# Norm's last step and the split of the score maxima on VectorE, earlier row loads and other turn slots in a four-layer FNet and sliding-window attention kernel

## Chip, cores and metric

One core of a Trainium2 chip. The metric is the device time of one execution in microseconds (us). The kernel before takes 2400.96 us, the median of 3 runs (2399.59 to 2403.11).

## What is computed

Four layers on x of 2048 rows by 640 columns, in fp32: FNet mixing, attention, FNet mixing, attention, each behind a layer norm and with a residual.

```python
def _A_ref(x, dft_seq_re, dft_seq_im, dft_hid_re, dft_hid_im):
    a = jnp.einsum("bsd,ed->bse", x, dft_hid_re)
    b = jnp.einsum("bsd,ed->bse", x, dft_hid_im)
    return jnp.einsum("ts,bse->bte", dft_seq_re, a) - jnp.einsum("ts,bse->bte", dft_seq_im, b)

def _B_ref(x, wqkv, wo):                      # H = 32 heads of 20, window W = 256
    ...
    scores = jnp.einsum("bhqd,bhkd->bhqk", q, k) * (Dh ** -0.5)
    mask = (idx[:, None] - idx[None, :] >= 0) & (idx[:, None] - idx[None, :] < W)
    p = _softmax(jnp.where(mask[None, None], scores, -1e9), axis=-1)
    o = jnp.einsum("bhqk,bhkd->bhqd", p, v)
    return (lambda x, *d: x.transpose(*d))(o, 0, 2, 1, 3).reshape(B, S, D) @ wo

x = x + _A_ref(_layernorm(x), ...)
x = x + _B_ref(_layernorm(x), B_wqkv, B_wo)
x = x + _A_ref(_layernorm(x), ...)
x = x + _B_ref(_layernorm(x), B_wqkv, B_wo)
```

## The kernel before

Products are made in fp16 on TensorE (PE), each fp32 operand split into a high and a low part, with three products for one. The FNet layers (`spectral`) take 0 to 605 us and 1290 to 1788 us. The change lies in the attention layers (`attention`), whose slots take 605 to 1232 us and 1788 to 2375 us.

**Slots.** An attention layer runs 256 slots g: 8 blocks of 256 rows (b), 32 slots r each; a slot is one tile of 128 query rows for one pair of heads. In slot g

- `scores(g)` (L1026) writes the scores of the slot to the bank `sp` (one buffer); VectorE (DVE) masks them (L1043) and takes the largest of each query into `m` (L1047).
- `by_key(g - 7)` (L1071) makes the scores of an earlier slot again, keys on the partitions, in the bank `tp` (one buffer); the largest scores come in as two more rows of the stack `qs`. ScalarE (ACT) takes the exponential into `ptq` (L1092); GpSimd (POOL) cuts the window's edges out (L1097, L1099).
- Every fourth slot: `values` multiplies by v, `back` (L1129) transposes and divides (L1140 to L1144).

**Maxima.** Of four slots 4n to 4n+3 one `m` holds the maxima. `part_tops(n)`, in slot 4n+4, splits them on GpSimd into a high and a low part in `tops` (L1053 to L1055). `hand_on(n)`, at the end of that slot, transposes `tops` on TensorE into the bank `pt`, and `copy_tops` has ScalarE copy that into rows of `qs` (L1069).

**Fill.** Between these stand the products of the projections and of the output (`proj_qk`, `proj_v`, `out_tile`, bank `pf`), cut to single matmuls. `run_fill(ns)` issues so many ns of them in a slot, by a rate that spreads the rest over the layer. A `turn` (`turned`, L936) is five transposes of a 128x640 tile into the bank `pt`, which has one buffer and is shared with `hand_on`, and a copy out of it by ScalarE (L947) or VectorE (L945). `turn_unit` issues at most one in a slot. `flush(kind)` issues all that is left of a kind at a deadline, and first ends the unit under way.

**Norms.** A norm (`norm_steps`, L118) is cut to steps of a few VectorE instructions; `slow_step` issues one in a slot, behind that slot's reduction (`tc.issue_after(topped[0])`). Its last step writes `lny` (L147); then `split` casts it on ScalarE (`xs`, L159) and takes the low part on GpSimd (L160). `rows_norm(b + 2)` makes so the rows that the projections of a later block read (two tiles, both layers, blocks 2 to 7); its rows are loaded from `x2_d` on SP's queue, in slot r = 13 (`VALUE_LAG`), just ahead of the first step. `next_norm` (first attention layer only) does the same for a finished output tile. Loads, and the stores of `qkd` with the loads of `qs` and `ks` behind them, share SP's queue, in order.

The order of each engine's instructions comes from the tile framework, from the order and the constraints of the code.

Of the kernel before, what the change touches and what calls it, by code (L numbers as in the profile page):

```python
# [42 lines left out]
HAND_LAG = 4  # L43
# [3 lines left out]
M_UP = 2.0 ** 15  # L47
SHIFT = -20.0
TURN_STEPS = 8
X_UP = 2.0 ** 10  # L50
C_UP = 2.0 ** 8
W_UP = 2.0 ** 13
# [6 lines left out]
def body(ctx: ExitStack, tc: tile.TileContext, x_in, cmat, whid, wqkv, wo, out):  # L59
# [55 lines left out]

    matmul, transpose = partial(tensor, "matmul"), partial(tensor, "transpose")

    def norm_steps(xs, ys, eng=nc.vector):  # L118

        n = len(xs)  # L120
        mv = keep.tile([P, n, 2], F32, tag=f"lnmv{n}", name="lnmv", bufs=2)
        for k, x in enumerate(xs):
            st = keep.tile([P, 2, 6], F32, tag="lnst", name="lnst", bufs=2)
            for h in range(2):
                nc.vector.bn_stats(st[:, h], x[:, h * 320:(h + 1) * 320])
                if h == 0:
                    yield
            nc.vector.bn_aggr(mv[:, k], st.rearrange("p a b -> p (a b)"))
            yield
        t = keep.tile([P, 3, n], F32, tag=f"lnt{n}", name="lnt", bufs=2)  # L130
        v, g, u = t[:, 0], t[:, 1], t[:, 2]
        nc.vector.tensor_scalar(v, mv[:, :, 1], 1e-5, X_UP ** -2, op0=OP.add, op1=OP.mult)
        nc.vector.tensor_scalar(g.bitcast(I32), v.bitcast(I32), 1, None, op0=OP.logical_shift_right)
        nc.vector.tensor_scalar(v, v, -0.5, None, op0=OP.mult)
        nc.vector.tensor_scalar(g.bitcast(I32), g.bitcast(I32), -1, 0x5F3759DF, op0=OP.mult, op1=OP.add)
        yield
        for k in range(3):
            if n == 1:
                nc.vector.scalar_tensor_tensor(u, g, v, g, op0=OP.mult, op1=OP.mult)
            else:  # L140
                nc.vector.tensor_tensor(u, g, g, op=OP.mult)
                nc.vector.tensor_tensor(u, u, v, op=OP.mult)
            nc.vector.scalar_tensor_tensor(g, u, 1.5, g, op0=OP.add, op1=OP.mult)
            yield
        for k, x in enumerate(xs):
            y = keep.tile([P, D], F32, tag="lny", name="lny", bufs=2)
            normed[0] = eng.tensor_scalar(y, x, mv[:, k, 0:1], g[:, k:k + 1],  # L147
                                                op0=OP.subtract, op1=OP.mult).ins
            ys.append(y)
            yield  # L150
# [608 lines left out]
    def attention(layer, proj, dst, final):  # L759
        with ExitStack() as st:  # L760
# [135 lines left out]

            def next_norm(i, x3):
                ys = []
                yield from norm_steps([x3], ys, nc.gpsimd)
                xs = new_xs()  # L900
                split(xs[:, 0], xs[:, 1], ys[0], nc.gpsimd)
                xt = keep.tile([P, 2, ND, P], F16, tag="xto", name="xto", bufs=2)
# [19 lines left out]
            def rows_norm(b, x2s):  # L922

                ys = []
                yield from norm_steps(x2s, ys, nc.gpsimd)
                for t, y in enumerate(ys):
                    xs = new_xs()
                    split(xs[:, 0], xs[:, 1], y, nc.gpsimd)
                    live[-1].extend(rows_turn(b, xs, t, k) for k in range(2))
                    fill.extend(Unit(now[0] + TURN_STEPS // 2, g, ("rows", b), now[0], [], True) for g in live[-1])  # L930
                    yield

            def rows_turn(b, xs, t, k):
# [75 lines left out]
                return sum(max(u.ns, 0) for u in fill + [unit[0]] if u is not None and u.kind in kinds) - credit[0]  # L1009

            def flush(kind):
                while any(u.kind == kind for u in fill) or (unit[0] and unit[0].kind == kind):
                    if unit[0] is None:
                        unit[0] = min((u for u in fill if u.kind == kind), key=lambda u: u.due)
# [34 lines left out]
            def part_tops(n):  # L1049

                m, hl = TOP.pop(n), tops[n % 2]
                u = sb.tile([P, 4, 2], F32, tag="u", name="u", bufs=2)
                nc.gpsimd.tensor_scalar(u, m, -1.0 / M_UP, None, op0=OP.mult)  # L1053
                nc.gpsimd.tensor_copy(hl[:, :, 0:66:64], u)
                nc.gpsimd.tensor_tensor(hl[:, :, 1:66:64], u, hl[:, :, 0:66:64], op=OP.subtract)  # L1055

            def hand_on(n):

# [135 lines left out]
            for g in range(NS):  # L1194
                now[0] = g
                b, r = divmod(g, 2 * NP)
                if g < NG:
                    if r == 0:
                        flush(("qk", b))
                        flush(("rows", b + 1))  # L1200
                        if b < NBQ - 1:
                            queue_qk(b + 1)
                            queue_v(b + 1)
                    scores(g)
                if 0 <= g - KEY_LAG < NG:
                    by_key(g - KEY_LAG)
                if g < NG and r == VALUE_LAG:
                    flush(("v", b))
                    if b < NBQ - 2:
                        proj.new_rows(b + 2)  # L1210
                        x2s = [keep.tile([P, D], F32, tag="res", name="x2", bufs=4) for t in range(2)]
                        for t in range(2):
                            load(x2s[t], x2_d[2 * (b + 2) + t])
                        slow.append(rows_norm(b + 2, x2s))
                    if b == NBQ - 1 and not final:
                        hidden = Hidden(xu_d)
                        hidden.load()
# [3 lines left out]
                for pi in range(2):  # L1221
                    n, m = divmod(g - HAND_LAG - 1 - pi, 4)
                    if m == 0 and 0 <= n < NG // 4:
                        copy_tops(n, pi)
                n, m = divmod(g - HAND_LAG, 4)
                if m == 0 and 0 <= n < NG // 4:
                    part_tops(n)
                slow_step()
                n, m = divmod(g - VALUE_LAG, 4)
                if m == 0 and 0 <= n < NG // 4:  # L1230
# [7 lines left out]
                    rate = max(rate, left(("v", b)) / (VALUE_LAG - r))  # L1238
                if g < NG and r < QK_SLOT:
                    rate = max(rate, left(("v", b), ("qk", b + 1)) / (QK_SLOT - r))  # L1240
                if (g - HAND_LAG) % 4 in (0, 3) or g >= NG + HAND_LAG:
                    turn_unit()
                run_fill(max(rate, 400) * FILL[(g - VALUE_LAG + 2) % 4])
                n, m = divmod(g - HAND_LAG, 4)
                if m == 0 and 0 <= n < NG // 4:
                    hand_on(n)
# [41 lines left out]
```

## Time and profile before

| | |
|---|---|
| runs, median of 3 | 2400.96 us |
| profiled execution, time | 2404.99 us |
| profiled execution, span of the core | 2403.3 us |
| mean granted TensorE clock over the span | 0.97 |
| GpSimd norm steps (L147) | 40, 102.3 us |
| GpSimd split of the maxima (L1053 to L1055) | 3 x 128, 31.0 + 27.1 + 28.6 us |
| ScalarE exponential (L1092) | 512, 486.2 us |

A profile line of a wait reads: who waited, for whom, us in total, how often, the longest. A line of the timeline reads: start, duration, engine, line, operation, tile written and tiles read, shapes, and in brackets how long the engine had been idle and what ended that. "PEld" is TensorE's weight load, "PEclk" the granted clock as a share of full speed. The lines of kernel.py that a profile names are those of the kernel before.

### The profile page before, as it was taken

The page shows a single profiled execution, that of the slowest core. Times are in us where ns is not written, and L with a number is a line of the kernel's source. Part 1 is how long each engine was busy: PE and PEld are TensorE (multiplying, and loading weights), DVE is VectorE, ACT ScalarE, POOL GpSimd, SP SyncE. Part 2 cuts the span into 40 slices and gives each one's busy share as a digit, 9 for nine tenths or more (in the row PEclk, how much of TensorE's full clock was granted, in tenths as well). Part 3 has the DMA queues.
Part 4 walks back from the last instruction along what each step waited for, and adds up shares of the span by engine and source line. Part 5 has one row for each costly group of instructions (what it writes and reads, how often), then busy time and mean ns, then how long its engine had stood idle before and what let it go on. Part 6 is the DMA issues. An engine that isn't in the chain of part 4 may idle for free.

```text
span 2403.3 us, 55464 instructions
## 1 busy us (share of the span) xinstructions
PE 2169.1 (90%) x21985; PEld 1515.7 (63%) x21985; DVE 1621.3 (67%) x3305; ACT 1267.7 (53%) x2120; POOL 1539.1 (64%) x2197
## 2 busy tenths in 40 slices
PE   7999899989898888889888999999987899889997
PEld 5667566667565566566556777777665566666664
DVE  7887979676666666666656758585766565656564
ACT  5334443432576666666654433434325666666775
POOL 5666758565557676666556858585746655665554
PEclk9999999999999999999898999999999999999999
DMA  5854556275330332133314545464542321232130
GB/s 179 287 203 157 200 176 204 90 255 140 95 86 31 83 96 63 49 91 85 128 57 141 192 136 192 136 202 169 197 109 68 85 56 56 70 85 62 53 90 23
DMA packets 187609, 292.98 MB, mean 122 GB/s; under 512 B 13908, under 2 KB 120660, under 8 KB 178004
## 3 DMA queue, kind: packets, MB, share of 16 engines
q1 hardware_dynamic: 157108, 223.55, 31.0%
q10 hardware_dynamic: 30240, 65.88, 7.4%
q8 instruction: 172, 2.82, 0.5%
q14 instruction: 89, 0.73, 0.1%
HBM read 202.51 MB, written 86.87 MB: 120 GB/s over the span
## 4 chain that ended last, share of the span: by engine, by line
PE 58%; DVE 17%; POOL 9%; DMA 7%; issue 5%; ACT 3%; SPq 0%; DVEq 0%; ACTq 0%; POOLq 0%
PE pf L112 23%; PE y L112 8%; PE pv L112 6%; PE z L112 6%; PE x L112 6%; DVE cc L482 5%; PE sp L112 4%; POOL lny L147 3%; DVE m L1047 2%; PE tp L112 2%; PE pt L112 2%; DVE sp L1043 2%; ACT ptq L1092 2%; DMA x<-x2d 1%; DVE res L505 1%
## 5 line engine op out<-in xcount | busy, mean ns | idle before, releaser
L112 PEld LDWEIGHTS <-cc 128*128 128x128 f16 x5376 | 528.0, 99 | 243.4 <-issue 38.8
L1092 ACT ACTIVATE ptq<-tp,shift,alpha 128x768 f32<-128x768 f32 (+2 forms) x512 | 486.2, 950 | 212.5 <-PE tp L112 199.5
L112 PEld LDWEIGHTS <-big 128*128 128x128 f16 x4320 | 413.2, 99 | 144.5 <-issue 31.1
L1043 DVE COPY_PREDICATED sp<-mask,sp 128x256 f32<-128x256 int32 x448 | 191.4, 427 | 292.4 <-PE sp L112 277.9
L1047 DVE TENSOR_REDUCE m<-sp 128x2 f32<-128x512 f32 (+1 forms) x512 | 344.8, 673 | 25.6 <-POOL os L1143 0.5
L1097 POOL TENSOR_SCALAR_AFFINE_SELECT ptq<-ptq 128x512 f32<-128x512 f32 x224 | 142.8, 637 | 284.3 <-ACT ptq L1092 274.3
L112 PE MATMUL pf<-early,big 128*128 128x256 f16 x2400 | 312.2, 277 | 1.1 <-ACT qf L328 1.1
L479 ACT ACTIVATE cc<-cs 128x512 f16<-128x512 f32 x256 | 152.3, 623 | 254.6 <-POOL cs L472 103.5
L112 PE MATMUL y<-zc,cc 128*128 128x320 f16 x1728 | 265.3, 301 | 13.7 <-DVE pf L505 13.7
L112 PE MATMUL pf<-big 128*128 128x320 f16 x1680 | 243.4, 303 | 12.2 <-DVE early L250 5.4
L482 DVE SCALAR_TENSOR_TENSOR cc<-cs,cc 128x512 f16<-128x512 f32 x256 | 232.3, 923 | 4.9 <-ACT cc L479 4.9
L482 DVE SCALAR_TENSOR_TENSOR cc<-cq,cc 128x512 f16<-128x512 f32 x192 | 201.2, 1049 | 0.0
L112 PE MATMUL pv<-ptq,v 128*32 128x128 f32 (+1 forms) x3840 | 191.2, 340 | 0.0
L112 PE MATMUL z<-zc,cc 128*128 128x320 f16 x1152 | 180.5, 302 | 8.4 <-DVE res L505 8.4
L112 PE MATMUL tp<-qs,ks 62*128 62x128 f16 x2688 | 153.9, 221 | 33.9 <-ACT ptq L1092 32.8
L1099 POOL TENSOR_SCALAR_AFFINE_SELECT ptq<-ptq 128x512 f32<-128x512 f32 x256 | 164.7, 643 | 29.1 <-ACT ptq L1092 28.3
L112 PE MATMUL x<-zc,cc 128*128 128x320 f16 x1152 | 182.7, 303 | 0.0
L112 PE MATMUL sp<-ks,qs 62*128 62x256 f16 (+1 forms) x1792 | 155.2, 252 | 29.3 <-DVE m L1047 28.1
L112 PEld LDWEIGHTS <-ks 62*128 62x128 f16 x3008 | 119.0, 96 | 82.4 <-issue 51.2
L112 PE MATMUL pf<-big,early 128*128 128x320 f16 x960 | 160.1, 308 | 3.7 <-DVE x L872 3.7
L1069 ACT ACTIVATE qs<-pt 2x512 f16<-2x512 f16 x224 | 131.4, 586 | 54.1 <-PE pt L112 50.4
L112 PEld LDWEIGHTS pv<-ptq,v 128*32 128x32 f32 x3840 | 110.4, 113 | 59.9 <-issue 8.2
(146 smaller groups left out, 3654.7 us busy)
## 6 DMA issues: line engine op xcount, KB each, us to landing
cq<-in_cmat_dram SPq DMA_DIRECT2D x64, 1024.0 KB
accd<-res ACTq DMA_DIRECT2D x96, 320.0 KB
res<-accd SPq DMA_DIRECT2D x96, 320.0 KB
x<-x2d SPq DMA_DIRECT2D x64, 320.0 KB
qkd<-early SPq DMA_DIRECT2D x160, 128.0 KB
ks<-qkd SPq DMA_DIRECT2D x108, 160.0 KB
qs<-qkd SPq DMA_DIRECT2D x84, 160.0 KB
x2d<-res ACTq DMA_DIRECT2D x32, 320.0 KB
```

What stands on the lines that cost most here:

```text
L112: i = getattr(nc.tensor, what)(*args, **kw)
L147: normed[0] = eng.tensor_scalar(y, x, mv[:, k, 0:1], g[:, k:k + 1], op0=OP.subtract, op1=OP.mult).ins
L479: nc.scalar.activation(cc[m][:, 0], f, AF.Copy, scale=C_UP)
L482: nc.vector.scalar_tensor_tensor(cc[m][:, 1], f, C_UP, cc[m][:, 0], op0=OP.mult, op1=OP.subtract)
L505: marks["dve"] = nc.vector.scalar_tensor_tensor(o, z, Y_DOWN, f, op0=OP.mult, op1=OP.add).ins
L1043: nc.vector.copy_predicated(sp[:, :, 2 * P:3 * P], mask[:, None, :].to_broadcast([P, 2, P]), far)
L1047: topped[0] = nc.vector.tensor_reduce(TOP[g // 4][:, g % 4], sp[:, :, c0:3 * P], axis=AX.X, op=OP.max).ins
L1069: nc.scalar.activation(o, handed[n][rs].rearrange("r (i p) t -> r i p t", i=2), AF.Copy)
L1092: nc.scalar.activation(q[:, h:h + 2, a0 + first:a0 + 3], tp[:, :, first * P:3 * P].rearrange("p a (b c) -> p a b c", c=P), AF.Sigmoid, bia ...
L1097: nc.gpsimd.affine_select(out=q[:, :, a0], in_=q[:, :, a0], pattern=[[0, 4], [-1, P]], base=0, channel_multiplier=1, compare_op=OP.is_gt, ...
L1099: ins = nc.gpsimd.affine_select(out=q[:, :, a0 + 2], in_=q[:, :, a0 + 2], pattern=[[0, 4], [1, P]], base=0, channel_multiplier=-1, compare ...
```

## The change

It has four parts.

- The last step of a norm (`lny`) is always VectorE's; in the attention layers it was GpSimd's.
- The maxima are split by two VectorE instructions, straight from `m`, in slot 4n+3 behind its reduction, where three GpSimd instructions did it in slot 4n+4. The steps of the norms wait for the second of them, too.
- The rows for `rows_norm` are loaded in slot r = 4 and not 13, and the norm starts in slot r = 9 and not 13. Their turns may come three and not four slots behind the norm.
- A turn is issued in slots 4n+3, and in slots 4n (in which `hand_on` follows) only if over 1000 ns of products come behind it; before in both. `flush` issues turns of the kind first, and does not end the unit under way for them.

```diff
+TURN_ROOM = 1000
+NORM_STEPS = (4, 9)
+ROW_STEPS = 3
...
-    def norm_steps(xs, ys, eng=nc.vector):
+    def norm_steps(xs, ys):
...
-            normed[0] = eng.tensor_scalar(y, x, mv[:, k, 0:1], g[:, k:k + 1],
+            normed[0] = nc.vector.tensor_scalar(y, x, mv[:, k, 0:1], g[:, k:k + 1],
                                                 op0=OP.subtract, op1=OP.mult).ins
...
-                yield from norm_steps([x3], ys, nc.gpsimd)
+                yield from norm_steps([x3], ys)
...
-                yield from norm_steps(x2s, ys, nc.gpsimd)
+                yield from norm_steps(x2s, ys)
...
-                    fill.extend(Unit(now[0] + TURN_STEPS // 2, g, ("rows", b), now[0], [], True) for g in live[-1])
+                    fill.extend(Unit(now[0] + ROW_STEPS, g, ("rows", b), now[0], [], True) for g in live[-1])
...
             def flush(kind):
+                for u in sorted((u for u in fill if u.kind == kind and u.turn), key=lambda u: u.due):
+                    fill.remove(u)
+                    while step(u):
+                        pass
                 while any(u.kind == kind for u in fill) or (unit[0] and unit[0].kind == kind):
...
                 m, hl = TOP.pop(n), tops[n % 2]
-                u = sb.tile([P, 4, 2], F32, tag="u", name="u", bufs=2)
-                nc.gpsimd.tensor_scalar(u, m, -1.0 / M_UP, None, op0=OP.mult)
-                nc.gpsimd.tensor_copy(hl[:, :, 0:66:64], u)
-                nc.gpsimd.tensor_tensor(hl[:, :, 1:66:64], u, hl[:, :, 0:66:64], op=OP.subtract)
+                hi = hl[:, :, 0:66:64]
+                nc.vector.tensor_scalar(hi, m, -1.0 / M_UP, None, op0=OP.mult)
+                topped[0] = nc.vector.scalar_tensor_tensor(hl[:, :, 1:66:64], m, -1.0 / M_UP, hi, op0=OP.mult, op1=OP.subtract).ins
...
                     scores(g)
+                    if g % 4 == 3:
+                        part_tops(g // 4)
                 if 0 <= g - KEY_LAG < NG:
                     by_key(g - KEY_LAG)
+                if g < NG and b < NBQ - 2:
+                    if r == NORM_STEPS[0]:
+                        x2s = [keep.tile([P, D], F32, tag="res", name="x2", bufs=4) for t in range(2)]
+                        for t in range(2):
+                            load(x2s[t], x2_d[2 * (b + 2) + t])
+                    if r == NORM_STEPS[1]:
+                        slow.append(rows_norm(b + 2, x2s))
                 if g < NG and r == VALUE_LAG:
                     flush(("v", b))
                     if b < NBQ - 2:
                         proj.new_rows(b + 2)
-                        x2s = [keep.tile([P, D], F32, tag="res", name="x2", bufs=4) for t in range(2)]
-                        for t in range(2):
-                            load(x2s[t], x2_d[2 * (b + 2) + t])
-                        slow.append(rows_norm(b + 2, x2s))
...
-                n, m = divmod(g - HAND_LAG, 4)
-                if m == 0 and 0 <= n < NG // 4:
-                    part_tops(n)
                 slow_step()
...
-                if (g - HAND_LAG) % 4 in (0, 3) or g >= NG + HAND_LAG:
+                ns = max(rate, 400) * FILL[(g - VALUE_LAG + 2) % 4]
+                m = (g - HAND_LAG) % 4
+                if m == 3 or m == 0 and credit[0] + ns > TURN_ROOM or g >= NG + HAND_LAG:
                     turn_unit()
-                run_fill(max(rate, 400) * FILL[(g - VALUE_LAG + 2) % 4])
+                run_fill(ns)
```

Three places of the program show how instructions move. The line numbers of the change's rows are its own.

**The norm of two tiles of rows, block 3 of the second attention layer.** GpSimd before (`x_27226` and `x_27227` are the rows, `qf` a projection's result):

```order
L329 CAST early<-qf 128x256
L147 TENSOR_SCALAR lny<-x_27226,lnmv,lnt 128x640
L330 TENSOR_TENSOR early<-qf,early 128x256
L147 TENSOR_SCALAR lny<-x_27227,lnmv,lnt 128x640
L160 TENSOR_TENSOR xs<-lny,xs 128x640 x2
L1097 AFFINE_SELECT ptq<-ptq 128x4x128
```

VectorE in the change, in the same block (`x_26713` and `x_26714` are the same rows):

```order
L150 TENSOR_SCALAR lny<-x_26713,lnmv,lnt 128x640
L1050 COPY_PREDICATED sp<-mask,sp 128x2x128
L1054 TENSOR_REDUCE m<-sp 128x2
L150 TENSOR_SCALAR lny<-x_26714,lnmv,lnt 128x640
L1050 COPY_PREDICATED sp<-mask,sp 128x2x128
L1054 TENSOR_REDUCE m<-sp 128x2
L1146 RECIPROCAL r<-pv 128x8
L1060 TENSOR_SCALAR tops_77<-m 128x4x2
L948 COPY ot<-pt 128x640
L1061 SCALAR_TENSOR_TENSOR tops_77<-m,tops_77 128x4x2
L1147 TENSOR_TENSOR o<-pv,r 128x160
```

The two steps `lny` leave GpSimd's queue and stand in VectorE's, one behind the reduction of a slot each, in two slots that follow each other. The last rows are a slot 4n+3, in which the two instructions on `tops` stand between the reduction and the next slot's masking copy, with those of `back` and a turn's copy among them.

**SP's queue around the load of rows, second attention layer.** Before (`x_27226`, `x_27227` are rows for a norm, `x_27321` a residual of an output tile, `qkd_1` the stores of k):

```order
L168 DMA qs<-qkd_0_153 20x16x256 x6
L168 DMA qkd_1_156<-early 128x2x256 x2
L168 DMA x_27226<-x2d_89 128x640
L168 DMA x_27227<-x2d_90 128x640
L168 DMA qkd_1_156<-early 128x2x256
L168 DMA x_27321<-x2d_83 128x640
```

In the change (`x_26713` and `x_26714` are those rows, `x_26676` and `x_27147` residuals):

```order
L171 DMA qs<-qkd_0_153 20x16x256 x6
L171 DMA x_26676<-x2d_82 128x640
L171 DMA x_26713<-x2d_89 128x640
L171 DMA x_26714<-x2d_90 128x640
L171 DMA qkd_1_156<-early 128x2x256 x3
L171 DMA x_27147<-x2d_83 128x640
```

The load of the rows stood behind the second store of k of its block, and now stands ahead of the first.

**TensorE in the first slot of block 4, second attention layer.** Before (`os` is a tile that is turned, `tops_78` the split maxima):

```order
L112 MATMUL pt<-idh,os 128x128
L112 LDWEIGHTS os
L112 MATMUL pt<-idh,os 128x128
L112 LDWEIGHTS tops_78
L112 MATMUL pt<-idh,tops_78 66x128
```

In the change (`early` are rows, `pf` the bank of a projection):

```order
L115 MATMUL pf<-big,early 128x320
L115 LDWEIGHTS early
L115 MATMUL pf<-big,early 128x320
L115 LDWEIGHTS tops_78
L115 MATMUL pt<-idh,tops_78 66x128
```

In before a turn stood directly ahead of the transposes of `tops`, and no product in that slot; in the change no turn stands in it and six products come ahead of them.

## Prediction

> **What bounds the kernel now.** I read the page first, for who is busy, and then the busy times by stretch, cut at the two attention layers (605 to 1232 us and 1788 to 2375 us) and the FNet layer between them.
>
> ```profile
> PE 2169.1 (90%) x21985; PEld 1515.7 (63%) x21985; DVE 1621.3 (67%) x3305; ACT 1267.7 (53%) x2120; POOL 1539.1 (64%) x2197
> ```
> ```profile
> core 0: us, PE busy (x) PEld busy (x) DVE busy (x) ACT busy (x) POOL busy (x), PEclk, DMA share, GB/s
> 605.00:1232.00 627.00, 546.84 (x7002) 373.89 (x7002) 408.89 (x1010) 412.90 (x622) 406.29 (x776) 0.96 0.28 78
> ...
> 1290.00:1788.00 498.00, 487.25 (x3615) 352.47 (x3614) 347.79 (x543) 187.27 (x377) 346.19 (x291) 1.00 0.51 170
> 1788.00:2375.00 587.00, 523.69 (x6761) 358.17 (x6760) 362.11 (x802) 387.16 (x578) 349.30 (x743) 0.96 0.25 66
> ```
>
> The FNet layer leaves TensorE (PE) idle for 498.0 - 487.3 = 11 us, at full clock. The attention layers leave it idle for 80 and 63 us, and there the granted clock is 0.96. The change touches the attention layers alone (the one shared function, `norm_steps`, is called elsewhere with VectorE already), so what it can gain lies in those 143 us and in the missing 0.04 of the clock. Next are TensorE's waits, first of 605 to 1232 us, then of 1788 to 2375 us (us in total, times, longest):
>
> ```profile
> PE sp L112 <- DVE m L1047: 17.7, 21, 2.3
> PE tp L112 <- ACT ptq L1092: 16.8, 16, 3.5
> PE pt L112 <- POOL tops L1055: 9.6, 9, 2.0
> PE pt L112 <- ACT xto L947: 7.3, 5, 3.4
> PE pt L112 <- DVE ot L945: 6.3, 5, 1.7
> PE pt L112 <- ACT xs L159: 5.7, 1, 5.7
> PE pt L112 <- ACT early L947: 4.1, 6, 1.1
> PE pt L112 <- ACT ot L947: 3.9, 5, 1.6
> ```
> ```profile
> PE sp L112 <- DVE m L1047: 21.0, 29, 2.2
> PE tp L112 <- ACT ptq L1092: 20.5, 10, 4.4
> PE pt L112 <- DVE ot L945: 5.4, 5, 1.1
> PE pt L112 <- POOL tops L1055: 5.4, 4, 4.3
> PE pt L112 <- DVE early L945: 2.8, 7, 0.6
> ```
>
> No single wait rules. There are four families: the bank `tp` that ScalarE (ACT) empties late, the bank `sp` that VectorE (DVE) empties late, the maxima that GpSimd (POOL) splits late, and the bank `pt` that holds a finished turn. To see why ScalarE is late I followed one of the longest, in the timeline of the second attention layer (TensorE, ScalarE, GpSimd):
>
> ```profile
> 2062.92 0.34 PE L112 MATMUL sp<-ks,qs 62*128 62x128 f16 x4
> 2066.94 0.50 PE L112 MATMUL tp<-qs,ks 62*128 62x128 f16 x6 [3.68 <-ACT ptq L1092]
> ```
> ```profile
> 2062.13 0.74 ACT L159 ACTIVATE xs<-lny 128x640 f16<-128x640 f32 x1 [1.61 <-POOL lny L147]
> ...
> 2065.27 0.74 ACT L159 ACTIVATE xs<-lny 128x640 f16<-128x640 f32 x1 [2.13 <-POOL lny L147]
> 2065.91 0.97 ACT L1092 ACTIVATE ptq<-tp,shift,alpha 128x768 f32<-128x768 f32 x1
> ```
> ```profile
> 2059.57 2.53 POOL L147 TENSOR_SCALAR lny<-x,lnmv,lnt 128x640 f32<-128x640 f32 x1
> ...
> 2062.72 2.52 POOL L147 TENSOR_SCALAR lny<-x,lnmv,lnt 128x640 f32<-128x640 f32 x1
> ```
>
> Read it from below. GpSimd takes 2.5 us for the last step of each of two norms. ScalarE's casts `xs` stand in its queue in front of the next exponential `ptq`, wait for both, and TensorE cannot write `tp` for 3.68 us. The stall costs more than itself, because the clock falls behind it:
>
> ```profile
> 2066.90:2070.30 3.40, 3.36 (x22) 2.51 (x22) 0.53 (x2) 1.96 (x3) 3.31 (x6) 0.51 0.02 5
> ```
> ```profile
> 2070.57 0.34 PE L112 MATMUL sp<-ks,qs 62*128 62x256 f16 x4
> ```
>
> For 3.4 us the clock is 0.51. The whole step, 2062.92 to 2070.57, is 7.65 us long. Taking 2.2 us for an ordinary step (256 steps in 587 us are 2.3 us with their stalls), 5.45 us are lost: 3.68 of waiting, 1.77 of half clock.
>
> **Last step of the norms to VectorE (forty instructions).** Their prices, on GpSimd and where VectorE already does them (ns: least, median, most):
>
> ```profile
> L147 POOL TENSOR_SCALAR lny<-x,lnmv,lnt x40: 2502/2520/3909, 646.1 to 2220.2; 128x640 f32<-128x640 f32 x40
> ...
> L147 DVE TENSOR_SCALAR lny<-xin,lnmv,lnt x16: 604/612/1553, 7.5 to 462.7; 128x640 f32<-128x640 f32 x16
> L147 DVE TENSOR_SCALAR lny<-x,lnmv,lnt x8: 599/1150/1685, 516.6 to 1754.6; 128x640 f32<-128x640 f32 x8
> ```
>
> I take 0.9 us, between the two medians, with ends of 0.6 and 1.7. Whom GpSimd holds up is in ScalarE's and VectorE's waits of the two layers (first layer, then second):
>
> ```profile
> ACT xs L159 <- POOL lny L147: 42.6, 22, 4.2
> ...
> DVE lnst L125 <- DMA x<-x2d: 13.8, 4, 4.0
> ```
> ```profile
> ACT xs L159 <- POOL lny L147: 20.7, 12, 2.1
> ...
> DVE lnst L125 <- DMA x<-x2d: 12.1, 5, 2.9
> ```
>
> Each norm becomes 2.5 - 0.9 = 1.6 us shorter, and by the order a step with its own `ptq` lies between two of them, so ScalarE no longer meets two waits in one step. Of TensorE's 16.8 + 20.5 = 37.3 us at `tp` I leave 10 and count **27 off** (18 if half of the waits stay, 37 if none does). GpSimd's second part `xs` stays where it is.
>
> **Maxima to VectorE (128 groups of four steps).** The three GpSimd instructions go, and the pair that replaces them stands behind the reduction one step earlier, so the transposes of `tops` find them done: of 9.6 + 5.4 = 15.0 us I count **14 off** (12 to 15).
>
> **What VectorE takes on.** No row has the pair's shape. The nearest small VectorE instructions are these (mean ns after the count):
>
> ```profile
> L143 DVE SCALAR_TENSOR_TENSOR lnt<-lnt 128x2 f32<-128x2 f32 x51 | 15.3, 299 | 1.3
> ...
> L134 DVE TENSOR_SCALAR lnt<-lnt 128x2 f32<-128x2 f32 x17 | 4.7, 275 | 0.5
> ```
>
> Together 0.57 us at most. These means hold some instructions that were held up, so I take 0.45, and 0.3 as the lower end. 128 x 0.45 + 40 x 0.9 = 58 + 36 = 94 us more on VectorE. It has (627 - 409) + (587 - 362) = 443 us idle there. The pair lies between one step's reduction and the next step's masking copy, whose `sp` TensorE needs a step later, so most of it falls in VectorE's idle time. In steps 4n+3, where the reciprocal and product of `back` and at times a statistics or a turn's copy also stand, it does not. I let 15 us of the 94 reach TensorE as waits at `sp` (0 to 48, half of it).
>
> **Rows loaded nine slots sooner, norm started four sooner.** In before the load is issued in the slot in which the norm begins, and VectorE's statistics wait for it with the next masking copy behind them:
>
> ```profile
> 2043.48 0.89 DVE L125 BATCH_NORM_STATS2 lnst<-x 128x6 f32<-128x320 f32 x2 [2.64 <-DMA x<-x2d]
> ```
> ```profile
> 2045.71 0.34 PE L112 MATMUL sp<-ks,qs 62*128 62x256 f16 x4 [1.87 <-DVE m L1047]
> ```
>
> 2.64 us on VectorE became 1.87 on TensorE, seven tenths. Of the 13.8 + 12.1 = 25.9 us that is 18; I count 15, because five slots (some 11 us) lie between load and use and SP's queue can still hold the load behind a `qkd` store. The load is moved ahead of those stores. It rewrites the buffers of the rows of the block before, which have been read long since, so it should hold nobody in the queue. So `sp`: 15 off, 15 on, **0**.
>
> **Turns only where products follow; turns first in a flush.** A turn leaves `pt` full, and the four transposes of `tops` wait for it if no product stands between. At a block's start before does exactly that, because the flush finishes a whole projection and the next slots have no credit left:
>
> ```profile
> 2090.59 0.38 PE L112 MATMUL pt<-idh,tops 128*66 128x128 f16 x4 [1.09 <-DVE ot L945]
> ```
>
> The order of the change has six products at that place. Turns within a flush still follow each other, and in the first layer the twelve turns of a block fill eight slots 4n+3 and spill to the next ones. Of 27.3 + 8.2 = 35.5 us at `pt` I count **12 off** (5 to 20). No work is dropped: the products are spread otherwise, and TensorE's tail after the last scores is the same.
>
> **Clock.** The missing 0.04 of 627 + 587 us is 48.6 us, or 28 stretches of 3.4 us at half. I let half of them go with their stalls, at the 1.8 us of the one priced above: 14 x 1.8 = **25 off** (6 to 20 stretches: 11 to 36). [...]
>
> **Sum.** 27 + 14 + 0 + 12 + 25 = 78 us. The profiled execution took 2404.99 us (span 2403.3 and 1.7 around it), so 2327 on its scale; the median of the runs, 2400.96, lies 4 us lower, and I give **2323**. The ends added up are 13 us (18 + 12 - 33 + 5 + 11) and 123 us (37 + 15 + 15 + 20 + 36). They don't fall together; 40 to 105 us, **2296 to 2361**, is what I expect 8 times in 10.
>
> **Rivals.** (1) ScalarE stays late. The new norm step stands behind VectorE's reduction and whatever is queued there, ScalarE's casts still stand in front of `ptq`, and half the waits at `tp` and most of their half clock remain: 10 us of the 27 and 15 of the 25 stay, 78 - 25 = 53 us are gained, 2348. For it: ScalarE waits in both layers whenever a norm ends. Against: one 2.5 us step becomes 0.9. (2) VectorE takes back what is gained. All of the 94 us reaches TensorE instead of 15, which is 79 us, and the time is 2402, no change. For it: VectorE is busy 65% in the first layer and would be at 78% of a shorter one. Against: it sits idle for a third of the layer now, and TensorE's present waits on it are 39 us, half of them a DMA's. (3) Slower: the pair is held by GpSimd. If each instruction of the pair waits out one of GpSimd's, the masking copy behind it and so `sp` come late in every group. Price: 0.45 us and a hold of 0.55 (the step from 0.612 to 1.150 us between the medians of VectorE's two sorts of norms), some 1 us in 128 groups, 128 us instead of 15: 113 - 78 = 35 us slower, 2436. It decides for slower from (78 + 15) / 128 = 0.73 us for a group on TensorE's path. For it speaks the 1553 ns against 612 of the same instruction. Against: the other reason to hold, GpSimd's own work, shrinks by the same forty steps of 2.5 us and 384 small ones. [...] That the change does not do what it says is excluded by the order.
>
> **Chances.** Forecast 0.76, rival 1 0.16, rival 2 0.04, rival 3 0.04. A measurement of this kernel tells 0.2% (5 us) from no change. So faster 0.92, same 0.04, slower 0.04. Rival 1's time lies within the range, which leaves out the two others and the ends of the forecast.
>
> **What would show it.** Right: GpSimd has no 128x640 norm step; ScalarE's waits before `xs` fall from 63 to under 25 us; TensorE's waits at `tp` to about 10 and at `tops` to about 1; VectorE's waits for x2d vanish; the granted clock of both layers is 0.98; VectorE's busy time is some 94 us larger and TensorE's wait at `sp` still near 39. Wrong: `sp` waits of 70 us or more (rivals 2, 3), pair instructions above 0.5 us each (rival 3), `tp` waits of 20 us or more (rival 1), or stalls at a block's start because the scores wait for `qs` or `ks`.

## The result, and the profile after

The change makes the kernel **faster: 2309.61 us** median of 4 runs (2304.6 to 2310.51) against 2400.28 us (2396.15 to 2403.11) of before on the same chip, a ratio of 0.9619 with a 95% interval of 0.9599 to 0.9639, or 90.7 us. The forecast was 2323 us, so it had 13 us too little of a gain. The profiled execution took 2304.60 us, the least of the four, with a span of 2302.9 us.

The page's first lines and the busy times by stretch stand against those of the prediction. First the page of after:

```profile
PE 2135.0 (93%) x21985; PEld 1499.2 (65%) x21985; DVE 1695.3 (74%) x3601; ACT 1264.4 (55%) x2120; POOL 1365.2 (59%) x1773
```

GpSimd (POOL) has 173.9 us less to do, VectorE (DVE) 74.0 us more. For the busy times by stretch I cut each trace at the first and the last masking copy of each attention layer, so that the cuts fit both programs. Before, then after:

```profile
core 0: us, PE busy (x) PEld busy (x) DVE busy (x) ACT busy (x) POOL busy (x), PEclk, DMA share, GB/s
606.30:1219.80 613.50, 536.75 (x6900) 367.49 (x6898) 399.84 (x976) 405.30 (x611) 397.11 (x753) 0.96 0.28 78
1791.30:2372.30 581.00, 518.59 (x6727) 355.33 (x6725) 359.66 (x797) 384.68 (x574) 346.41 (x724) 0.96 0.25 66
```
```profile
600.50:1166.50 566.00, 524.79 (x6910) 362.09 (x6910) 444.89 (x1141) 405.53 (x612) 302.65 (x539) 0.98 0.32 86
1731.20:2271.40 540.20, 506.45 (x6727) 349.28 (x6726) 389.02 (x934) 382.15 (x574) 279.78 (x523) 0.98 0.28 70
```

The two layers lose 47.5 + 40.8 = 88.3 us. TensorE's idle time (length less busy) falls from 76.8 + 62.4 = 139.2 us to 41.2 + 33.8 = 75.0, which is 64.2 us. Its busy time falls by 24.1 us for the same work (10 matmul records more in the first stretch): that is the clock, which was at half for 92.2 us of the two layers before and for 37.5 after. The rest of the spans' difference of 100.4 us lies outside these two stretches (5.8 us ahead of the first, 6.8 between them, half a microsecond given back at the end).

TensorE's waits in after, first layer and second layer (us in total, times, longest):

```profile
PE sp L115 <- DVE m L1054: 13.7, 25, 1.1
PE pt L115 <- DVE xto L948: 9.5, 8, 2.3
...
PE tp L115 <- ACT ptq L1098: 1.1, 4, 0.4
```
```profile
PE sp L115 <- DVE m L1054: 13.2, 27, 1.0
PE sp L115 <- DMA qs<-qkd: 7.3, 3, 5.6
PE sp L115 <- DMA x<-x2d: 3.9, 1, 3.9
...
PE tp L115 <- ACT ptq L1098: 1.4, 6, 0.4
...
PE pt L115 <- DVE tops L1061: 0.2, 1, 0.2
```

The bank that ScalarE empties late (`tp`) went from 36.0 to 2.5 us and the maxima from 15.0 to 0.4. Two rows of the second layer are new: the scores wait for a load of `qs` and, by the releaser that the trace infers, for one of rows. The scores do not read those rows; the loads of `qs` for that block stand directly ahead of them in SP's queue, so both rows are likely the same kind of stall. ScalarE's own waits for the norm, in the two layers, were 42.6 and 20.7 us:

```profile
ACT xs L162 <- DVE lny L150: 14.0, 23, 1.2
```
```profile
ACT xs L162 <- DVE lny L150: 6.2, 11, 1.0
```

The prices of the moved instructions (ns: least, median, most). The pair costs 0.35 us by its medians, the norm's step 0.735 where it was 2.520 on GpSimd:

```profile
L150 DVE TENSOR_SCALAR lny<-x,lnmv,lnt x48: 600/735/1685, 513.8 to 2115.0; 128x640 f32<-128x640 f32 x48
```
```profile
L1060 DVE TENSOR_SCALAR tops<-m x128: 170/181/1387, 606.6 to 2272.6; 128x8 f16<-128x8 f32 x128
L1061 DVE SCALAR_TENSOR_TENSOR tops<-m,tops x128: 164/172/1316, 606.8 to 2273.2; 128x8 f16<-128x8 f32 x128
```

The longest of the new waits sits at the start of block 4 of the second layer. On SP's queue the six loads of `qs` take 11.17 us to issue, 8.8 of them in a wait for a store of the output. TensorE stalls 5.59 us for these loads, and from 1992.8 us, 0.8 us into the stall, the clock is at 0.50 for 10.2 us:

```profile
1978.25 11.17 SPq L171 DMA_DIRECT2D qs<-qkd  x6
1989.51 1.43 SPq L171 DMA_DIRECT2D x<-x2d  x3
```
```profile
SPq L171 <- DMA out_dram<-x: 8.8, 1, 8.8
```
```profile
1997.55 0.37 PE L115 MATMUL sp<-ks,qs 62*128 62x256 f16 x2 [5.59 <-DMA qs<-qkd]
```
```profile
1992.80:2003.00 10.20, 5.45 (x53) 3.45 (x57) 2.24 (x4) 3.15 (x4) 1.22 (x2) 0.50 0.59 110
```

### The profile page after: what moved, and what is told of

Same layout as the page of the kernel before. It is cut to its first block, busy times and chain, and to the rows that moved or that the text cites. A ratio compares the mean times of both kernels' runs of the same rounds, so it can differ in the third digit from the quotient of the medians.

```text
span 2302.9 us, 55101 instructions
## 1 busy us (share of the span) xinstructions
PE 2135.0 (93%) x21985; PEld 1499.2 (65%) x21985; DVE 1695.3 (74%) x3601; ACT 1264.4 (55%) x2120; POOL 1365.2 (59%) x1773
## 4 chain that ended last, share of the span: by engine, by line
PE 64%; DVE 20%; DMA 5%; issue 5%; ACT 3%; POOL 2%; SPq 0%; DVEq 0%; ACTq 0%; POOLq 0%
PE pf L115 25%; PE y L115 9%; PE pv L115 8%; PE z L115 6%; PE x L115 6%; PE sp L115 5%; DVE cc L485 5%; DVE m L1054 3%; PE tp L115 3%; DVE sp L1050 2%; PE pt L115 2%; DMA qs<-qkd 1%; DVE res L508 1%; ACT ptq L1098 1%; DVE lnt L146 1%
## 5 line engine op out<-in xcount | busy, mean ns | idle before, releaser
L115 PE MATMUL pf<-early,big 128*128 128x256 f16 x2400 | 304.6, 273 | 0.0
L1075 ACT ACTIVATE qs<-pt 2x512 f16<-2x512 f16 x224 | 130.9, 585 | 39.7 <-PE pt L115 36.8
L115 PE MATMUL pf<-bo,ot 128*128 128x320 f16 x840 | 144.3, 304 | 6.7 <-DVE ot L948 6.5
```

The costliest lines, as they stand in the source:

```text
L115: i = getattr(nc.tensor, what)(*args, **kw)
L1075: nc.scalar.activation(o, handed[n][rs].rearrange("r (i p) t -> r i p t", i=2), AF.Copy)
```

## The experiments

The change has four parts: **norms** (last step to VectorE), **tops** (parts of the largest scores to VectorE, a step sooner), **rows** (loads nine slots sooner, norm four slots sooner, turns due a slot sooner) and **turns** (turns only where products follow, flush by due time). Eight of the twelve kernels take parts out of after or put parts into before; the other four split or double something. My theory was that what counts is whom TensorE waits for, wait by wait, with the clock behind the waits. The main rival was that GpSimd's relief as such is worth the time, wherever it comes.

This table holds all of them. Ratios are to before on the same chip. The columns of waits are TensorE's, summed over the rows of the two layers in us (the `pt` column is without `tops`); idle is the two layers' length less TensorE's busy time; half clock is the time in both layers for which the trace has the clock at 0.5. Half clock is of one execution each, and varies by chance: ahead of the first layer, where the programs are the same, it is 23.9 us in before and 13.7 in after. Over the twelve runs of the kernel with the tops alone the granted clock of the span is 0.963 to 0.972, which is 178 to 133 us at half (twice the missing share of the span).

| kernel | ratio (95% interval) | tp | sp, VectorE | sp, DMA | tops | pt | idle | half clock |
|---|---|---|---|---|---|---|---|---|
| before | 1 | 36.0 | 38.7 | 0 | 15.0 | 38.5 | 139.2 | 92.2 |
| norms | 0.9727 (0.9702 to 0.9752) | 2.0 | 36.4 | 0 | 10.4 | 32.3 | 91.0 | 54.6 |
| tops | 0.9955 (0.9936 to 0.9973) | 37.0 | 38.8 | 1.0 | 0 | 36.0 | 124.6 | 102.4 |
| turns | 0.9969 (0.9951 to 0.9986) | 41.9 | 36.8 | 0.3 | 14.8 | 18.6 | 127.8 | 81.9 |
| norms, rows | 0.9582 (0.9555 to 0.9608) | 2.5 | 18.6 | 0 | 7.4 | 30.2 | 66.7 | 37.6 |
| after (all four) | 0.9619 (0.9599 to 0.9639) | 2.5 | 27.3 | 11.7 | 0.4 | 23.0 | 75.0 | 37.5 |
| after less norms | 0.9839 (0.9810 to 0.9868) | 47.0 | 21.2 | 11.8 | 0 | 14.9 | 102.7 | 61.4 |
| after less tops | 0.9596 (0.9567 to 0.9625) | 2.2 | 20.0 | 10.5 | 8.9 | 22.9 | 72.9 | 30.7 |
| after less rows | 0.9662 (0.9635 to 0.9689) | 2.1 | 40.6 | 1.8 | 0.2 | 21.4 | 82.4 | 41.0 |
| after less turns | 0.9600 (0.9571 to 0.9629) | 2.7 | 27.9 | 0 | 0.4 | 29.9 | 70.7 | 35.2 |
| norms, rows, norm begun late | 0.9607 (0.9584 to 0.9630) | 1.8 | 21.1 | 0 | 10.6 | 28.7 | 68.7 | 47.8 |
| norms, rows, GpSimd's tops sooner | 0.9575 (0.9554 to 0.9597) | 2.3 | 21.3 | 0 | 5.8 | 30.2 | 67.5 | 30.7 |
| after, pair issued twice | 0.9781 (0.9755 to 0.9806) | 1.0 | 40.9 | 13.4 | 6.1 | 33.6 | 105.8 | 37.5 |
| after, second output tile sooner | 0.9570 (0.9547 to 0.9593) | 4.0 | 23.2 | 0 | 0.4 | 23.7 | 59.2 | 55.8 |

**After less the norms' part.** The edit gives the two callers in the attention layers their engine back:

```
-                yield from norm_steps([x3], ys)
+                yield from norm_steps([x3], ys, nc.gpsimd)
...
-                yield from norm_steps(x2s, ys)
+                yield from norm_steps(x2s, ys, nc.gpsimd)
```

> After with the norms' last step of the attention layers back on GpSimd (40 instructions of 2.5 us instead of 0.74 on VectorE); the other three parts stay. My theory (what counts is whom TensorE waits for): its waits at tp come back from 2.5 us to 25 to 37, ScalarE's waits before xs from 20 to about 60, and a part of the half-clock stretches behind them; less VectorE work gives back 5 us or less at sp. The time goes up by 30 to 50 us, to 2340 to 2360. Rival (GpSimd's load as such: the 174 us of busy time that it lost are spread evenly over the gain of 91): its 100 us here are worth 52 us. Rival (VectorE's load costs more than TensorE's present wait at sp shows): the time stays or falls, 2300 to 2315.

Measured: 2362.92 us, ratio 0.9839, some 53 us above after. The waits at `tp`, first layer and second layer:

```profile
PE tp L115 <- ACT ptq L1098: 27.4, 25, 3.4
```
```profile
PE tp L115 <- ACT ptq L1098: 19.6, 9, 4.3
```

They come back to 47.0 us, and ScalarE waits for GpSimd's norms again (42.8 and 19.9 us). The size is a little above my range, and it is also what the rival said (52); the next kernel parts the two.

**After less the tops part.** The edit:

```
-                hi = hl[:, :, 0:66:64]
-                nc.vector.tensor_scalar(hi, m, -1.0 / M_UP, None, op0=OP.mult)
...
+                nc.gpsimd.tensor_scalar(u, m, -1.0 / M_UP, None, op0=OP.mult)
+                nc.gpsimd.tensor_copy(hl[:, :, 0:66:64], u)
...
-                    if g % 4 == 3:
-                        part_tops(g // 4)
```

> After with the parts of the largest scores back on GpSimd (three small instructions per group, one step later); the other parts stay. My theory: TensorE's waits at tops come back from 0.2 us to 10 to 15, hardly any clock with them since each is short (0.3 us or less), and VectorE's 45 us less give back 3 to 8 us at sp. The time goes up by 5 to 15 us, to 2315 to 2325. Rival (GpSimd's load as such): GpSimd gets 73 of its 174 us back, which are 38 us of the gain: 2348. Rival (VectorE's pair costs most of its 45 us): faster, 2275 to 2300.

Measured: 2307.34 us, ratio 0.9596, no slower than after as far as the two intervals can tell. So the rival falls: GpSimd took 78 us of busy time back (1365.2 to 1443.1 on the page) and it cost nothing. My 5 to 15 us fell too. Of the 15.0 us at `tops` 8.9 came back (first layer, then second):

```profile
PE pt L115 <- POOL tops L1062: 3.1, 4, 1.7
```
```profile
PE pt L115 <- POOL tops L1062: 5.8, 6, 1.5
```

In the first layer that is a third of the 9.6 us of before: GpSimd's norm steps, which stood in front of the three instructions, are gone. In the second layer it is all of the 5.4. VectorE's `sp` wait fell by 7.3 us. The two nearly cancel.

**After less the rows part.** The edit puts the load and the norm's start back to slot 13:

```
-                    if r == NORM_STEPS[0]:
-                        x2s = [keep.tile([P, D], F32, tag="res", name="x2", bufs=4) for t in range(2)]
...
-                    if r == NORM_STEPS[1]:
-                        slow.append(rows_norm(b + 2, x2s))
```

> After with the row loads issued where the norm begins again, and the norm started four slots later; the other parts stay. My theory: VectorE's waits for x2d come back (0 to about 26 us), seven tenths of them reach TensorE at sp, and some half clock: the time goes up by 15 to 25 us, to 2325 to 2335. Rival (GpSimd's load as such): no change, 2305 to 2315, since no instruction changes its engine. Rival (the norm's start in slot 9 is what makes turns ready in time, and without it ScalarE's chain ends late again): the waits at tp come back too, 10 us or more.

Measured: 2321.99 us, ratio 0.9662, 10 us slower than after. VectorE's waits for rows return, and with them TensorE's at `sp` (first layer of this kernel):

```profile
PE sp L113 <- DVE m L1052: 19.8, 29, 2.1
```
```profile
DVE lnst L126 <- DMA x<-x2d: 7.2, 3, 2.7
```

`sp` is 13.3 us more, but the new waits for DMA (11.7 in after) go down to 1.8. The part is worth more than 10 us; in after it also brings a stall. `tp` stays at 2.1, so the earlier norm is not what freed ScalarE.

**After less the turns part.** The edit:

```
-                for u in sorted((u for u in fill if u.kind == kind and u.turn), key=lambda u: u.due):
...
-                if m == 3 or m == 0 and credit[0] + ns > TURN_ROOM or g >= NG + HAND_LAG:
+                if (g - HAND_LAG) % 4 in (0, 3) or g >= NG + HAND_LAG:
...
```

> After with the old rule for turns (in steps 4n and 4n+3 whatever follows, and flushes by due time); the other parts stay. My theory: TensorE's waits at pt grow by 10 to 15 us, and the new stalls of 11 us at the second layer's block starts for qs and for a residual row (which the later second output turn made) vanish: between no change and 10 us slower, 2305 to 2320. If those stalls come from the loads moved ahead and not from the turns, they stay, and it is 12 to 17 us slower. Rival (GpSimd's load as such): no change.

Measured: 2305.6 us, ratio 0.9600, again no slower as far as the intervals can tell. The second layer is 7.9 us shorter than in after (532.3), with no row for `qs` or `x2d` left; the first is 3.2 us longer. So the turns' rule takes 7 us of `pt` waits away and, beside the rows part, makes the stall at the block's start.

**The norms' part alone in before.** The edit is the first one's opposite:

```
-                yield from norm_steps([x3], ys, nc.gpsimd)
+                yield from norm_steps([x3], ys)
```

> Before with the norms' last step of the attention layers moved to VectorE, and nothing else. Taking it out of after cost 53 us of the 91 while the other three parts taken out singly cost 12 at most together, so parts must cover for each other. My theory (the chain norm, casts, turned copies at tp is the one that TensorE waits for longest, and the rest hides behind it): tp falls from 37 to under 5 us, sp, tops and pt stay near 39, 15 and 35, and the time falls by 50 to 65 us, ratio 0.973 to 0.979. Rival (VectorE's load, 29 us more here, is only affordable because the loads come earlier): 20 to 40 us, ratio 0.983 to 0.992. Rival (the norm's step is nearly all): 80 us or more, ratio under 0.967.

Measured: 2338.23 us, ratio 0.9727, 65.6 us faster, the edge of my range. `tp` is 2.0 us, and `tops`, of which no instruction changed, is down by 4.6 us in all:

```profile
PE tp L112 <- ACT ptq L1092: 1.0, 4, 0.4
PE pt L112 <- POOL tops L1055: 2.1, 3, 1.0
```
```profile
PE tp L112 <- ACT ptq L1092: 1.0, 3, 0.4
PE pt L112 <- POOL tops L1055: 8.3, 6, 2.6
```

The fall at `tops` is the first layer's (9.6 to 2.1); in the second layer it rose (5.4 to 8.3), and why it did no run shows.

**Norms and rows.** Before with these two parts:

```
+                    if r == NORM_STEPS[0]:
...
+                            load(x2s[t], x2_d[2 * (b + 2) + t])
+                    if r == NORM_STEPS[1]:
+                        slow.append(rows_norm(b + 2, x2s))
```

> Before with two parts: the norms' last step on VectorE, and the rows loaded and their norm started sooner. If the parts for the largest scores and for the turns are each worth nothing because they do nothing here, this is after: ratio 0.960 to 0.963. My theory (tops and turns both remove waits of TensorE before the same transposes of tops, and each alone is enough): neither is worth anything with the other there, but with both gone it is 10 to 25 us slower than after, ratio 0.966 to 0.972.

Measured: 2303.1 us, ratio 0.9582. My theory, that the lack of both other parts would cost 10 to 25 us, is wrong: **these two parts are the whole gain**, and the other two on top of them bring nothing, if anything a loss of 9 us (0.0037, at the edge of what the two intervals can tell). `sp` in the two layers:

```profile
PE sp L114 <- DVE m L1049: 9.1, 12, 1.1
```
```profile
PE sp L114 <- DVE m L1049: 9.5, 21, 1.1
```

From norms alone to norms and rows that is 36.4 to 18.6, 17.8 us, and half clock falls by a further 17.0 us, which chance alone could give. In after `sp` is 27.3: with the pair it is 7 to 9 us more (20.0 and 18.6 without it).

**Tops alone, and turns alone, in before.** The edits are the opposites of the second and the fourth:

```
+                nc.vector.tensor_scalar(hi, m, -1.0 / M_UP, None, op0=OP.mult)
...
-                nc.gpsimd.tensor_copy(hl[:, :, 0:66:64], u)
```
```
+                if m == 3 or m == 0 and credit[0] + ns > TURN_ROOM or g >= NG + HAND_LAG:
```

> Before with the parts of the largest scores moved to VectorE one step sooner, and nothing else. My theory: TensorE's 15 us at tops vanish, but VectorE's 45 us more put up to 7 us back at sp (taking the part out of after lowered sp from 27 to 20 us): 5 to 15 us faster, ratio 0.994 to 0.998. Rival (VectorE's small instructions cost more, since its waits for rows and GpSimd's norms are still there): no change or slower, ratio 0.999 to 1.01. Rival (GpSimd's relief as such speeds its norms up, and with them tp): 20 us or more, ratio under 0.992.

> Before with the new rule for turns and flushes, and nothing else. Taking it out of after gained 3 us in the first layer's favour and cost 8 in the second's disfavour: the stall for qs that it makes there. My theory: 12 us off at pt and tops, less up to 11 us of that stall: no change to 10 us faster, ratio 0.996 to 1.001. Rival (the new rule is what brings turns and products apart whatever the engines do): 12 us or more faster, ratio under 0.995.

Measured: tops 2390.52 us, ratio 0.9955 (10.8 us), turns 2394.65 us, ratio 0.9969 (7.4 us), both inside my ranges. TensorE's idle time falls with tops by 14.6 us, nearly the wait removed, but the half clock does not follow (102.4 against 92.2 us, a difference within chance). `sp` stays as it was, 38.8 against 38.7 us, though VectorE has the pair here. With turns `pt` falls by 20 us and `tp` rises by 6; I read this as a wait that is partly met again at the next bank, which no run shows.

**Slot or engine for the tops.** Norms and rows, with GpSimd's three instructions issued one step sooner:

```
                     scores(g)
+                    if g % 4 == 3:
+                        part_tops(g // 4)
...
-                n, m = divmod(g - HAND_LAG, 4)
-                if m == 0 and 0 <= n < NG // 4:
-                    part_tops(n)
```

> Two parts of the change (norms' last step on VectorE; rows and norms sooner, ratio 0.9582) and the parts of the largest scores left on GpSimd but issued one step sooner, where the change has them on VectorE. It asks whether the slot or the engine removed TensorE's waits at tops (15.0 us before, 7.4 us with the two parts, 0.2 after). My theory (the slot does; the pair on VectorE is what raised sp from 19 to 27 us): tops falls under 2 us, sp stays at 17 to 21, and the time falls by 3 to 8 us, ratio 0.955 to 0.957, the fastest so far. Rival (the engine does: GpSimd is late with the three instructions because of what stands before them, so a step more helps little): tops 4 to 7 us, ratio 0.957 to 0.960.

Measured: 2302.51 us, ratio 0.9575. The first layer's wait falls to 1.1 us, the second's stays:

```profile
PE pt L114 <- POOL tops L1057: 1.1, 1, 1.1
```
```profile
PE pt L114 <- POOL tops L1057: 4.7, 6, 1.1
```

In all 5.8 us against 7.4, which is the rival's number: one slot sooner on GpSimd does not end these waits, and VectorE one slot sooner does. It does not matter for the time.

**Load or norm.** Norms and rows, with the load early and the norm begun late:

```
-NORM_STEPS = (4, 9)
-ROW_STEPS = 3
+NORM_STEPS = (4, 13)
+ROW_STEPS = 4
```

> The same two parts, with the row loads at slot 4 but the norm begun in slot 13 and its turns due as before. It splits the part on the rows: on top of the norms' step it gave 35 us, of which TensorE's wait at sp accounts for 18. My theory (the early load does it, since VectorE's wait for x2d is what goes): ratio 0.957 to 0.962. Rival (the norm's earlier start does it, by ending the turns' chain ahead of the block's end): 15 to 30 us slower than the two parts, ratio 0.965 to 0.971.

Measured: 2308.44 us, ratio 0.9607, as my theory had it. `sp` is 21.1 us against 18.6, so the early load is what counts for most of it; whether the norm's earlier start is worth anything (0.0025) the intervals leave open.

**The pair twice.** After with both instructions of the pair repeated:

```
+                for _ in range(2):
                     nc.vector.tensor_scalar(hi, m, -1.0 / M_UP, None, op0=OP.mult)
...
```

> After with VectorE's pair of instructions for the largest scores issued twice (the same values written again): 128 pairs of 0.35 us, 45 us more on VectorE, nothing else changed. It measures what VectorE's idle time still covers. My theory (the first 45 us raised TensorE's wait at sp by 8 us and the rest is covered): sp rises from 27 to 35 to 50 us, the time by 8 to 25 us, ratio 0.965 to 0.972. Rival (the cover is used up): 35 us or more slower, ratio 0.976 or above.

Measured: 2347.59 us, ratio 0.9781, 39 us above after (0.0162 of 2400). I was wrong and the rival right: by the medians 45 us were added, and VectorE's busy time on the page grew by 58.3 (1695.3 to 1753.6). Busy times of this kernel in the two layers:

```profile
602.90:1190.60 587.70, 526.94 (x6912) 362.10 (x6914) 477.54 (x1268) 406.77 (x612) 303.72 (x539) 0.99 0.30 83
1757.30:2310.00 552.70, 507.64 (x6727) 347.90 (x6725) 412.69 (x1061) 383.96 (x574) 280.16 (x523) 0.98 0.27 68
```

TensorE idles 105.8 us, 30.8 more, with VectorE busy for only 78% of the two layers (890 of 1140 us). The waits grow at `sp` (27.3 to 40.9), `pt` (23.0 to 33.6) and `tops` (0.4 to 6.1). The first pair in each group is nearly covered; the second costs 39 / 128 = 0.30 us, of 0.35 by its medians or 0.46 by the busy time. Less than half of the 30.8 us stands at `sp`.

**The second output tile sooner.** After with one number of the planner's table changed:

```
-OUT_STEPS = (4, 2, 8)
+OUT_STEPS = (4, 2, 4)
```

> After with the second output tile of a block set four slots after the first and not eight, in the planner's table. In after the second residual load of a block stands behind the qs loads on SP's queue, and in the second layer TensorE waits 7.3 us for qs and 3.9 us for that row at block starts. My theory (the order of that load and store against the qs loads makes these stalls): they vanish, and the time falls by 8 to 12 us, ratio 0.957 to 0.959. Rival (they come from the turns of the rows that now end earlier, whatever the output does): they stay, and the ratio is 0.961 to 0.964.

Measured: 2297.38 us, ratio 0.9570, some 12 us faster than after. It is level with the kernel that has norms, rows and GpSimd's tops sooner (0.9575): even with this number changed, all four parts give no more than the two. The `qs` loads of block 4 now take 3.37 us to issue, not 11.17, the wait for the store stands behind them (6.8 us ahead of the loads of rows), and no row for `qs` or `x2d` is among TensorE's waits:

```profile
1996.72 3.37 SPq L171 DMA_DIRECT2D qs<-qkd  x6
2006.99 0.83 SPq L171 DMA_DIRECT2D x<-x2d  x2
```

SP's queue waits for stores of the output as long as ever (second layer, after, then this kernel). What changed is which loads stand behind such a wait.

```profile
SPq L171 <- DMA out_dram<-x: 47.2, 6, 8.8
```
```profile
SPq L171 <- DMA out_dram<-x: 46.9, 6, 10.2
```

## Why the prediction was right, and where it was not

**Sign and mechanism were right.** Waits of TensorE were to fall by 53 us and the clock to give 25; in the layers idle time fell by 64.2 us and busy time by 24.1. Of the named signs, `tops`, ScalarE's waits (20 us), VectorE's vanished waits for x2d and the clock of 0.98 came out as listed, and `tp` fell further than listed (2.5 us, not 10). Two did not: VectorE's busy time grew by 74.0 us and not 94, because the prices came out at 0.35 and 0.735 us where I took 0.45 and 0.9, and `sp` is 27.3 us and not near 39. One sign of being wrong came too, the stall for `qs` at a block's start.

**The norms' term was too small.** I took 27 us at `tp`; with this part alone it is 34.0 us. The same edit gave 4.6 us at `tops`, all of it in the first layer, where GpSimd's long step had stood in front of those instructions, and about 6 at `pt`. Idle time fell by 48.2 us and half clock by 37.6 us. In all it is worth 65.6 us, where I gave 27 and a share of the clock's 25.

**"15 off, 15 on, 0" at `sp` was the step that failed most.** The rows' load is worth 17.8 us at `sp`, near my 15, but 35 us of time on top of the norms (0.9727 to 0.9582; idle time falls by 24.3 us), where I had counted nothing net. What I set against it, 15 of VectorE's 94 us, was too much: the 74 us that VectorE did take on go with 7 to 9 us at `sp`. They don't add up from single parts. Taken out of after, the pair gives 7.3 us back and the norms' steps 6.1 (21.2 without them); put alone into before, neither raises `sp` (38.8 and 36.4 against 38.7). My argument by VectorE's idle share (443 us free) was no argument: with the pair twice VectorE still idles for 250 us of the two layers, and the second pair is paid all the same. That the cover which counts is the one between a reduction and the next masking copy fits this, but no run shows it. That the pair stayed on the cheap side of that limit was luck.

**The tops' 14 us were counted as wait, not as time.** The wait went (15.0 to 0.4), but a third of it the norms' part had removed already, and the pair's 7.3 us at `sp` pay for most of the rest: with the other parts there, no gain that the intervals show.

**The turns' 12 us came with a stall.** `pt` outside `tops` is 15.5 us lower in after, but 6 of that belong to the norms' part; the turns' rule takes 7 us there and, together with the early rows, puts the `qs` loads behind a wait for an output store: 11.7 us, and 10.2 us at half clock at the start of block 4. The prediction named stalls for `qs` at a block's start as a sign of being wrong, but gave them no term. That turns this part from a small gain (7.4 us alone) to none.

So the nearness of the sum was luck in part: two parts that I undervalued (norms, rows) made up for two that are worth nothing here (tops, turns).

**Rivals.** ScalarE did not stay late (`tp` 2.5 us). VectorE did not take it all back, and the pair was not held in most groups: its two medians are 0.181 and 0.172 us, and 10 of the 256 instructions took over 1 us. Each of these ten began while a GpSimd step `xs` (L163) ran and ended some 0.04 us after it, here one of 1.38 us:

```profile
1826.26 1.39 POOL L163 TENSOR_TENSOR xs<-lny,xs 128x640 f16<-128x640 f32 x1
1826.31 1.38 DVE L1060 TENSOR_SCALAR tops<-m 128x8 f16<-128x8 f32 x1
```

The rival of the slower side needed 0.73 us a group on TensorE's path; doubling the pair put 0.30 there.

**The clock.** After has 7 half-clock stretches in the two layers against 21, and 37.5 us at half against 92.2. Only two of the 7 have a single wait as long as the shortest stretch (3.41 us) beside them (5.59 us for `qs`, 3.95 at the next block's start), and these stretches begin 0.8 and 3.2 us after the wait began. What precedes all of them is idle time added up. All stretches begin on one grid of 3.41 us; in the 3.41 us ahead of each of these 28 TensorE was idle for 1.5 to 3.4 us in all, in 9 of them in two or more waits of over 0.1 us. The windows of that grid in the same layers behind which the clock stayed full hold 1.84 us or less. So waits of 1 to 2 us were followed by half clock here, alone (1.60 us ahead of the stretch at 1186.3 us in before) or close together (1.09 and 0.44 us ahead of that at 1125.8 us in after), and the clock's term had a cause: it was 24.1 us.

## What to carry to other kernels

Add up the waits of the engine that bounds the time, but do not add the gains of edits that remove neighbouring waits: the long GpSimd step in front of others caused waits in three rows (ScalarE's `xs`, TensorE's `tp` and, in the first layer, `tops`), and once it and the late loads were gone the edits made for `tops` and `pt` were worth nothing. Don't judge a helper engine's room by its idle share: 0.35 us more in a group was nearly free and the next 0.35 cost 0.30, with the engine idle for a fifth of the time. Double the new instructions to learn how much room is left. After moving loads in a shared queue, look at what the queue's waits now stand in front of; one number of the output's schedule gave 12 us back.

## What the runs showed of the hardware

The half-clock stretches of the two layers have lengths of 3.41, 6.83 or 10.24 us in before and after, multiples of one step, and in each trace they begin on one grid of that step. TensorE was idle for 1.53 us or more in the window of that grid ahead of each of the 28, and for 1.84 us or less in each of the 602 whole windows that had full clock and were followed by it. The two ranges overlap, so these traces show no sharp bound. The time at half clock varies with the execution: ahead of the first attention layer, where the programs are the same, it is 23.9 us in before and 13.7 in after, and that layer starts between 600.5 and 608.6 us in the fourteen traces. So two profiled executions are to be compared layer by layer; the 100.4 us between the two spans hold 12 us from outside the layers, where 53 us were at half clock before and 30 after, and the medians differ by 90.7 us.

Loads on SP's queue waited for a store that another engine issued: in the second layer the queue waits in all 32.0 us in before, 47.2 in after, 45.5 with norms and rows, 48.3 in after less the turns and 46.9 in the last kernel for `out_dram`, which is on ScalarE's queue, by the releaser that the trace infers. Why a load needs that store's end no run shows.
